# Folding the last two weights later, and splitting in halves, in a fused attention, gated MLP and bilinear MLP kernel

## The chip, the cores and the metric

The kernel runs on one core of one Trainium2 chip. The metric is the device time of one execution in microseconds (us); lower is better. A run's time is the median of several executions. A profile is one execution more, recorded instruction by instruction; its own time stands beside its span.

## The reference

```python
attn_out = _attn_ref(q, k, v)              # 4 batches, 8 heads, 576 positions, head size 64, window 128
x = attn_out.transpose(0, 2, 1, 3).reshape(2304, 512)
gate = 1.0 / (1.0 + np.exp(-(x @ w_gate))) # w_gate, w_val: 512 x 1536
x = gate * (x @ w_val) @ w_out             # w_out: 1536 x 512
a, b = x @ w1, x @ w2                      # w1, w2: 512 x 1024
h = a * b @ w3                             # w3: 1024 x 1024
out = h @ w_out2                           # w_out2: 1024 x 512
```

All data is float32. The weights reach the kernel as float64 words and are rounded to float32 on the chip.

## The kernel before, in words

**Split operands.** Each matrix product is three TensorE passes over values split into a high part (a rounded copy that ScalarE makes, `act_copy`) and a low part (the rest). The low part is a subtraction on VectorE (`dve_lo`) or on GpSimd (`pool_lo`, line 86). A group "wsl", "gt", "tp", "tq", "t", "forms" or "xf" in the profile is such a pair.

**Stages.** From 0 to some 190 us the attention runs, with the first products of the first MLP laid between as fillers. Then the first MLP runs group by group: a group is two slices of 128 hidden columns, and for each group all five token blocks (128 or 512 tokens wide parts of `TILES`) are passed: `gv` makes gate and value products in four PSUM banks, ScalarE's tanh (line 337) reads the first two banks, VectorE's product (line 344, "g") reads the other two, and `down1` ("dn") multiplies by `w_out` one block later.

**The last group.** The last group passes the blocks in the order `LAST_ORDER`. After each block `FOLD_PLAN` says in letters what else is recorded: `c` converts one more weight piece, `f` records one unit of the fold, `x` one step of `x_forms`. The fold computes w3 times w_out2 once (16 units of 12 matmuls, "w3o", line 285), so that the second MLP needs one product less. `x_forms` makes sums and differences of the tokens of two blocks ("xf"): with them seven block products do the work of eight. The weight forms ("forms") are made per slice from 12 on in `form_sink`.

**Weights on their way.** A piece is loaded (`fetch`, "raw", two buffers in turn), rounded from float64 by one ScalarE and six VectorE instructions (`rounded`, lines 131 to 137), and either split into its place or, for pieces of `early`, stored to DRAM as float32 ("early32") and loaded again later at half the bytes. `W3_AHEAD` and `W3_LATER` name the pieces of w3 that go that way. Rounding buffers ("ca") come two in turn too, so a piece waits for the store of the piece before last.

**Second MLP.** For eight slices (12 to 19) and two pairs of blocks, `products` makes the seven products in two PSUM banks "pb" and "pd" and one "pc"; ScalarE copies partial sums out of "pb" (x, xa, xb) before TensorE may add to them again; `lone` does the block that has no pair. The forms of each slice are stored to DRAM by line 214 ("formd") on SyncE's queue and loaded again for the second pair.

**What sets the order.** Each engine runs its own list in order; the lists are made by a scheduler from the recorded program, its priorities and its own estimate of times. TensorE's, VectorE's and ScalarE's lists interleave the stages; a row in a list waits for its data and for the buffer it writes, and everything behind it on that engine waits too. DMA issues are rows of the list of the engine that issues them.

Of the kernel before, what the change touches and what calls it, by code (L numbers as in the profile page):

```python
# [9 lines left out]
F32 = mybir.dt.float32  # L10
# [3 lines left out]
AF = mybir.ActivationFunctionType  # L14
ALU = mybir.AluOpType
# [4 lines left out]
P = 128  # L20
# [14 lines left out]
FULL = 4000.0  # L35

LAST_ORDER = (4, 0, 1, 2, 3)
FOLD_PLAN = {4: "ccccc", 0: "ccc", 1: "cccccccccc", 2: "cfcfcfcf", 3: "cfxcfxcfxx", None: "xxxffccfccfcfcfcfcfcf"}

PAIRED = ((1, 2), (3, 4))  # L40
A21, A22, A11, A12, S1, S2, S3, S4 = range(8)
# [4 lines left out]
)  # L46

W3_AHEAD = (0, 1, 10, 11, 12, 13, 14, 15)
W3_LATER = (2, 3, 4, 5)


def bits(word):
# [4 lines left out]
def attn_moe_kernel(  # L57
# [14 lines left out]
    nc = tc.nc  # L72
    NPAIR = qt.shape[0]
    D = P // 2
    NF, NM, NC2 = w_gate.shape[0], w1.shape[0], w_out2.shape[0]
# [3 lines left out]
    def act_copy(dst, src):  # L79
        nc.scalar.activation(dst, src, AF.Copy)  # L80
# [2 lines left out]
        nc.vector.tensor_tensor(dst, src, hi.bitcast(F32), ALU.subtract)  # L83

    def pool_lo(dst, src, hi):
        nc.gpsimd.tensor_tensor(dst, src, hi.bitcast(F32), ALU.subtract)  # L86

    aligned = ctx.enter_context(tc.tile_pool(name="aligned", bufs=1, side="right"))
    aligned.tile([P, 8], F32, name="aligned")
# [5 lines left out]
    formd = dpool.tile([NM * P, 7 * 4 * P], F32, name="formd")  # L95
    outd = dpool.tile([NM * P, 2 * DM], F32, name="outd")
# [87 lines left out]
    forms = {}  # L184
# [3 lines left out]
    def form_sink(key, x):  # L188

        i, c = key  # L190
        x = x.rearrange("p (b c) -> p b c", b=2)
        if c == 0:
            forms[i] = formpools[i % 2].tile([P, 8, 2, 2 * P], F32R, name=f"forms{i}", tag=f"forms{i % 2}")
            half[i] = x
        w = forms[i]

        def split(at, src):
            hi, lo = w[:, at : at + 2, 0], w[:, at : at + 2, 1]
            act_copy(hi, src)
            pool_lo(lo, src, hi)  # L200

        split(A11 if c == 0 else A21, x)
        if c == 1:
            a = half.pop(i)
            s12 = spool.tile([P, 2, 2 * P], F32, name=f"s12_{i}", tag="cs")
            s34 = spool.tile([P, 2, 2 * P], F32, name=f"s34_{i}", tag="cs")
            nc.vector.tensor_tensor(s12[:, 0], x[:, 0], x[:, 1], ALU.add)
            nc.vector.tensor_tensor(s12[:, 1], s12[:, 0], a[:, 0], ALU.subtract)
            nc.vector.tensor_tensor(s34[:, 0], a[:, 0], x[:, 0], ALU.subtract)
            nc.vector.tensor_tensor(s34[:, 1], a[:, 1], s12[:, 1], ALU.subtract)  # L210
            split(S1, s12)
            split(S3, s34)
            r = (i - NF) * P
            nc.sync.dma_start(formd[r : r + P, :], w[:, 1:].rearrange("p b h c -> p (b h c)").bitcast(F32))

    def out_tile(i):
        if i % GF == 0:
# [46 lines left out]
    early += [((i, c), (w1, w2)[c][i - NF]) for i in groups[NF // GF + 2] for c in range(2)]  # L264
    early += [it for it in fold_src if it[0][0] == "w3" and it[0][1] in W3_LATER]
    late_n = len(early)
# [6 lines left out]
    def fold_items():  # L273
        sinks = dict(o2=wo2_sink, w3=w3_sink)
        return [(key, ahead.get(key, src), sinks[key[0]]) for key, src in fold_src]

    def fold():
        for u in range(2 * NM):
            m, c = divmod(u, 2)
            if c == 0:  # L280
                acc2 = mm_tile([P, DM], f"w3o{m}")
            for i in range(4):
                kk = 4 * c + i
                for wp, xp in PASSES:
                    nc.tensor.matmul(  # L285
                        acc2, w3s[u][:, wp, i * P : (i + 1) * P], wo2[kk][:, xp],
                        start=(kk == 0 and wp == 0 and xp == 0),
                        stop=(kk == NC2 - 1 and wp == 1),
                    )
            if c == 1:  # L290
                o = m2.tile([P, 2, DM], F32R, tag="gt", name=f"w3o{m}", bufs=4)
                nc.scalar.activation(o[:, 0], acc2, AF.Copy, scale=0.25)
                nc.vector.scalar_tensor_tensor(o[:, 1], acc2, 0.25, o[:, 0].bitcast(F32), ALU.mult, ALU.subtract)
                nc.sync.dma_start(outd[m * P : (m + 1) * P, :], o.rearrange("p h c -> p (h c)").bitcast(F32))
            yield


# [7 lines left out]
    def mm_tile(shape, name):  # L305
        mmturn[0] += 1
        return mmpools[mmturn[0] % len(mmpools)].tile(shape, F32, tag="mm", name=name)
# [81 lines left out]
    def x_forms(n):  # L389

        p, q = (acc[blk] for blk in PAIRED[n])
        b11, b21, b12, b22 = p[:, 0:2], p[:, 2:4], q[:, 0:2], q[:, 2:4]

        def split(j, src, lo):
            t = xf[n, j] = xpool.tile([P, 2, 2, TB], F32R, name=f"xf{n}_{j}", tag=PLACES[n][j])
            act_copy(t[:, 0], src)
            lo(t[:, 1], src, t[:, 0])

        def minus(to, x, y):
            nc.vector.tensor_tensor(to, x, y, ALU.subtract)  # L400

        split(B11, b11, pool_lo)
        yield
        split(B21, b21, pool_lo)
        yield
        split(B22, b22, dve_lo)
        yield
        minus(b12, b12, b11)
        split(T1, b12, pool_lo)
        yield  # L410
        minus(b22, b22, b12)
        split(T2, b22, dve_lo)
        yield
        minus(b11, b22, b11)
        split(T3, b11, pool_lo)
        yield
        minus(b21, b21, b22)
        split(T4, b21, dve_lo)
        yield
# [437 lines left out]
    for blk in LAST_ORDER:  # L857
        for _ in layer(groups[last1], blk):
            pass
        follow(FOLD_PLAN[blk])  # L860
    flush()
# [7 lines left out]
    queue[2:2] = first[0:2]  # L869
    follow(FOLD_PLAN[None])  # L870
    assert not queue and next(fold_it, None) is None
# [7 lines left out]
    def step(it):  # L879
        return next(it, None)  # L880

    downs = iter(())
    for n in range(len(PAIRED)):
        for g, grp in enumerate(second):
            final = n == 0 and g + 1 == len(second)
            for at, i in enumerate(grp):
                alone = lone(i) if n == 0 else iter(())
                if i == slices[-1] and n == 0:
                    xform = x_forms(1)
                for gap in products(n, i):  # L890
                    if gap:
                        step(downs)
                    if gap in (2, 3):
                        step(alone)
                    if i == slices[-1] and n == 0:
                        step(xform)
                if at:
                    for _ in downs:
                        pass
                convert(2)  # L900
                nxt = n * len(slices) + slices.index(i) + 2 - len(slices)
                if 0 <= nxt < len(slices):
                    again(slices[nxt])
            nxt = n * len(second) + g + 1
            if nxt < 2 * len(second):
                out_again(second[nxt % len(second)])
            downs = down2(n, grp)
            if final:
                for _ in range(5):
                    step(downs)  # L910
# [53 lines left out]
```

## Time and profile before

| | |
|---|---|
| median of 3 runs | 927.54 us (925.88 to 927.7) |
| the profiled execution | 927.45 us, its span 925.7 us |
| TensorE busy | 880.0 us, 95% of the span |
| VectorE, ScalarE, GpSimd busy | 667.7, 352.0 and 330.0 us |
| chain that ended last | TensorE 61%, VectorE 20%, DMA 6%, ScalarE 5%, GpSimd 4% |
| mean granted TensorE clock | 0.989 of full speed |

The profiled execution is 0.09 us below the median of the runs, so sums made from its rows are set against 927.45. The 1.75 us between the span and its time lie around the program.

### The profile page before, as it was taken

The page shows a single profiled execution, that of the slowest core. Times are in us where ns is not written, and L with a number is a line of the kernel's source. Part 1 is how long each engine was busy: PE and PEld are TensorE (multiplying, and loading weights), DVE is VectorE, ACT ScalarE, POOL GpSimd, SP SyncE. Part 2 cuts the span into 40 slices and gives each one's busy share as a digit, 9 for nine tenths or more (in the row PEclk, how much of TensorE's full clock was granted, in tenths as well). Part 3 has the DMA queues.
Part 4 walks back from the last instruction along what each step waited for, and adds up shares of the span by engine and source line. Part 5 has one row for each costly group of instructions (what it writes and reads, how often), then busy time and mean ns, then how long its engine had stood idle before and what let it go on. Part 6 is the DMA issues. An engine that isn't in the chain of part 4 may idle for free.

```text
span 925.7 us, 12453 instructions
## 1 busy us (share of the span) xinstructions
PE 880.0 (95%) x4432; PEld 716.4 (77%) x4432; DVE 667.7 (72%) x1126; ACT 352.0 (38%) x839; POOL 330.0 (36%) x360
## 2 busy tenths in 40 slices
PE   6778998999999999999999999989899999999998
PEld 4556775788878888888888888867688888888886
DVE  5979898538997995896798844972679956434444
ACT  6878666532323322422332333432443324122120
POOL 4767554542323312412411213230755446112121
PEclk9999899999999999999999999999999999999999
DMA  5445352133241341251235332237644432555332
GB/s 198 154 134 184 109 191 78 38 91 115 91 154 63 103 161 44 82 161 65 69 128 167 114 91 95 65 114 265 235 171 183 192 126 93 217 212 188 108 114 91
DMA packets 40622, 121.66 MB, mean 131 GB/s; under 512 B 4464, under 2 KB 6512, under 8 KB 38512
## 3 DMA queue, kind: packets, MB, share of 16 engines
q1 hardware_dynamic: 40416, 120.74, 38.1%
q8 instruction: 35, 0.57, 0.3%
q14 instruction: 27, 0.22, 0.1%
q10 hardware_dynamic: 144, 0.13, 0.0%
HBM read 88.34 MB, written 32.51 MB: 131 GB/s over the span
## 4 chain that ended last, share of the span: by engine, by line
PE 61%; DVE 20%; DMA 6%; ACT 5%; issue 4%; POOL 4%; SPq 0%; ACTq 0%; DVEq 0%; POOLq 0%
PE gv L320 22%; PE dn L361 11%; PE o L519 9%; PE pb L429 7%; PE pd L429 3%; PE w3o L285 2%; ACT sm L682 2%; PE pc L429 2%; DVE s L666 1%; DVE sm L669 1%; PE lone L493 1%; PE pv L723 1%; DVE mn L675 1%; DVE acc L400 1%; POOL wsl L86 1%
## 5 line engine op out<-in xcount | busy, mean ns | idle before, releaser
L320 PE MATMUL gv<-xth,wsl 128*128 128x512 f32 (+1 forms) x960 | 282.3, 372 | 1.7 <-DVE g L344 1.0
L320 PEld LDWEIGHTS gv<-xth,wsl 128*128 128x128 f32 x960 | 176.3, 191 | 37.0 <-issue 3.0
L320 PE MATMUL gv<-xtl,wsl 128*128 128x512 f32 (+1 forms) x480 | 177.9, 371 | 0.2 <-DVE xtl L83 0.2
L361 PE MATMUL dn<-gt,wsl 128*128 128x512 f32 (+1 forms) x720 | 157.4, 372 | 12.1 <-DVE xtl L83 5.3
L86 POOL TENSOR_TENSOR gt<-g,gt 128x512 fp32r<-128x512 f32 (+1 forms) x60 | 74.6, 1247 | 239.2 <-ACT gt L80 239.0
L361 PEld LDWEIGHTS dn<-gt,wsl 128*128 128x128 f32 x720 | 126.6, 190 | 37.7 <-issue 6.2
L320 PEld LDWEIGHTS gv<-xtl,wsl 128*128 128x128 f32 x480 | 91.6, 191 | 15.5 <-DVE xtl L83 0.9
L371 DVE TENSOR_TENSOR acc<-acc,dn 128x512 f32<-128x512 f32 (+1 forms) x120 | 73.0, 625 | 15.6 <-PE dn L361 15.6
L529 DVE TENSOR_TENSOR acc<-acc,o 128x512 f32<-128x512 f32 x54 | 36.9, 684 | 49.0 <-PE o L519 49.0
L80 ACT ACTIVATE gt<-g 128x512 fp32r<-128x512 f32 (+1 forms) x60 | 35.1, 587 | 78.6 <-DVE g L344 78.5
L682 ACT ACTIVATE sm<-sm,mn 128x128 f32<-128x128 f32 x144 | 55.8, 390 | 18.1 <-DVE mn L679 13.0
L344 DVE SCALAR_TENSOR_TENSOR g<-g,gv 128x512 f32<-128x512 f32 (+1 forms) x60 | 37.3, 627 | 29.8 <-PE gv L320 27.4
L429 PE MATMUL pb<-xf,forms 128*128 128x512 f32 x192 | 50.7, 396 | 4.4 <-ACT xa L80 4.3
L86 POOL TENSOR_TENSOR tp<-x,tp 128x512 fp32r<-128x512 f32 x16 | 21.3, 1334 | 93.5 <-ACT tp L80 61.7
L429 PE MATMUL pb<-xf,again 128*128 128x512 f32 x192 | 49.5, 393 | 0.0
L519 PE MATMUL o<-outw,tp 128*128 128x512 f32 x192 | 48.4, 391 | 0.7 <-POOL tp L86 0.7
L519 PE MATMUL o<-outw,tq 128*128 128x512 f32 x192 | 48.7, 391 | 0.0
L690 POOL TENSOR_SCALAR sm<-sm,su 128x128 f32<-128x128 f32 x72 | 32.4, 463 | 43.1 <-DVE su L686 35.8
L285 PE MATMUL w3o<-wo,w3s 128*128 128x512 f32 x192 | 46.4, 398 | 0.7 <-ACT w3s L80 0.7
L429 PEld LDWEIGHTS pb<-xf,forms 128*128 128x128 f32 x192 | 34.8, 188 | 12.2 <-ACT xa L80 4.9
L285 PEld LDWEIGHTS w3o<-wo,w3s 128*128 128x128 f32 x192 | 36.3, 190 | 10.0 <-ACT w3s L80 1.1
L337 ACT ACTIVATE g<-gv 128x512 f32<-128x512 f32 (+1 forms) x60 | 32.2, 544 | 30.5 <-PE gv L320 26.8
(804 smaller groups left out, 1561.1 us busy)
## 6 DMA issues: line engine op xcount, KB each, us to landing
formd<-forms SPq DMA_DIRECT2D x8, 1792.0 KB, 6.1
outw<-outd SPq DMA_DIRECT2D x16, 512.0 KB, 5.0
again<-formd SPq DMA_DIRECT2D x8, 1024.0 KB, 5.2
ldk<-in_k_dram SPq DMA_DIRECT2D x16, 320.0 KB, 3.9
ldv<-in_v_dram SPq DMA_DIRECT2D x16, 320.0 KB, 3.0
out_dram<-acc SPq DMA_DIRECT2D x18, 256.0 KB, 2.0
ldq<-in_q_dram SPq DMA_DIRECT2D x16, 256.0 KB, 4.1
outd<-w3o SPq DMA_DIRECT2D x8, 512.0 KB, 2.9
```

The costliest lines, as they stand in the source:

```text
L80: nc.scalar.activation(dst, src, AF.Copy)
L86: nc.gpsimd.tensor_tensor(dst, src, hi.bitcast(F32), ALU.subtract)
L285: nc.tensor.matmul(acc2, w3s[u][:, wp, i * P : (i + 1) * P], wo2[kk][:, xp], start=(kk == 0 and wp == 0 and xp == 0), stop=(kk == NC2 - 1 ...
L320: nc.tensor.matmul(ps, wsl[i][:, s, wp, kk * P : (kk + 1) * P], xs[blk][xp][:, kk], start=(kk == 0 and wp == 0 and xp == 0), stop=(kk == N ...
L344: nc.vector.scalar_tensor_tensor(pr, pr, 1.0, pss[i, 1], ALU.add, ALU.mult)
L361: nc.tensor.matmul(ps, wsl[i][:, 2, wp, m * P : (m + 1) * P], t[:, xp], start=n == 0, stop=n == 3 * len(grp) - 1,)
L371: nc.vector.tensor_tensor(a, a, ps, ALU.add)
L429: nc.tensor.matmul(ps, forms[i][:, a, wp, kk * P : (kk + 1) * P], xf[n, j][:, xp, kk], start=first and kk == 0 and (wp, xp) == PASSES[0], ...
L519: nc.tensor.matmul(ps, ts2[n, i][blk][:, xp, tt * P : (tt + 1) * P], outw[i][:, wp], start=k == 0, stop=k == 3 * len(grp) - 1,)
L529: nc.vector.tensor_tensor(a, a, ps, ALU.add)
L682: s["act"] = nc.scalar.activation(y, y, AF.Exp, bias=mn[:, j : j + 1], scale=1.0 / up, accum_out=su[:, j : j + 1])
L690: nc.gpsimd.tensor_scalar(y, y, su[:, j : j + 1], 1.0, ALU.mult, ALU.mult)
```

## The change

Five edits. `pool_lo` makes each GpSimd subtraction as two instructions over half the columns. Four more pieces of w3 (6 to 9) are rounded ahead, stored and loaded again, and `FOLD_PLAN` places conversions and fold units later: no fold unit stands any more between the third and the fourth wide block of the last group. `x_forms` works in halves of 512 columns, on all engines. The store of a slice's forms is issued from ScalarE's queue, after the fold's last copy (`folded`), when the slice's products are recorded. The store of a folded piece ("outd") is recorded one unit later.

```diff
-FOLD_PLAN = {4: "ccccc", 0: "ccc", 1: "cccccccccc", 2: "cfcfcfcf", 3: "cfxcfxcfxx", None: "xxxffccfccfcfcfcfcfcf"}
+FOLD_PLAN = {4: "cccc", 0: "cc", 1: "cccc", 2: "cccccccccccc", 3: "cfcfcfcfxxx", None: "xxxxfccfccfcfcfcfcfcfcfcfcff"}
...
-W3_LATER = (2, 3, 4, 5)
+W3_LATER = (2, 3, 4, 5, 6, 7, 8, 9)
...
     def pool_lo(dst, src, hi):
-        nc.gpsimd.tensor_tensor(dst, src, hi.bitcast(F32), ALU.subtract)
+        n = src.shape[1] // 2
+        for k in (slice(0, n), slice(n, 2 * n)):
+            nc.gpsimd.tensor_tensor(dst[:, k], src[:, k], hi[:, k].bitcast(F32), ALU.subtract)
...
             split(S3, s34)
-            r = (i - NF) * P
-            nc.sync.dma_start(formd[r : r + P, :], w[:, 1:].rearrange("p b h c -> p (b h c)").bitcast(F32))
+
+    def keep(i):
+        r = (i - NF) * P
+        nc.scalar.dma_start(formd[r : r + P, :], forms[i][:, 1:].rearrange("p b h c -> p (b h c)").bitcast(F32))
...
-                nc.scalar.activation(o[:, 0], acc2, AF.Copy, scale=0.25)
+                folded[m] = nc.scalar.activation(o[:, 0], acc2, AF.Copy, scale=0.25)
...
-                nc.sync.dma_start(outd[m * P : (m + 1) * P, :], o.rearrange("p h c -> p (h c)").bitcast(F32))
+                made.append((m, o))
+            if c == 0 or u == 2 * NM - 1:
+                for k, o in made:
+                    nc.sync.dma_start(outd[k * P : (k + 1) * P, :], o.rearrange("p h c -> p (h c)").bitcast(F32))
...
-            act_copy(t[:, 0], src)
-            lo(t[:, 1], src, t[:, 0])
+            for h in range(2):
+                act_copy(t[:, 0, h], src[:, h])
+                lo(t[:, 1, h], src[:, h], t[:, 0, h])
...
-            nc.vector.tensor_tensor(to, x, y, ALU.subtract)
+            for h in range(2):
+                nc.vector.tensor_tensor(to[:, h], x[:, h], y[:, h], ALU.subtract)
...
+                if n == 0:
+                    with tc.issue_after(folded[NM - 1].ins):
+                        keep(i)
```

What the edits make of the lists shows at three places. (Numbers behind a name are buffers.)

The first place is ScalarE's list after the last group's first block (block 4). "a_" is the first instruction of a rounding, g_4 the tanh of that block, gt_4 the high part of its product. Before:

```order
L131 ACTIVATE a_('ahead', 'w3', 5)_5073<-raw_('ahead', 'w3', 5)_5059 128x512
L337 ACTIVATE g_4_4823<-gv_4_0_4797 128x512
L337 ACTIVATE g_4_4825<-gv_4_0_4810 128x512
L80 ACTIVATE gt_4_4840<-g_4_4823 128x512
L80 ACTIVATE gt_4_4857<-g_4_4825 128x512
L80 ACTIVATE wo_0_5191<-raw_('o2', 0)_5071 128x512
L80 ACTIVATE wo_0_5191<-raw_('o2', 1)_5083 128x512
L337 ACTIVATE g_0_4979<-gv_0_0_4953 128x256
```

After:

```order
L133 ACTIVATE a_('ahead', 'w3', 6)_5283<-raw_('ahead', 'w3', 6)_5269 128x512
L348 ACTIVATE g_4_4909<-gv_4_0_4883 128x512
L348 ACTIVATE g_4_4911<-gv_4_0_4896 128x512
L133 ACTIVATE a_('ahead', 'w3', 7)_5295<-raw_('ahead', 'w3', 7)_5281 128x512
L80 ACTIVATE gt_4_4926<-g_4_4909 128x512
L133 ACTIVATE a_('ahead', 'w3', 8)_5405<-raw_('ahead', 'w3', 8)_5293 128x512
L80 ACTIVATE gt_4_4944<-g_4_4911 128x512
L133 ACTIVATE a_('ahead', 'w3', 9)_5417<-raw_('ahead', 'w3', 9)_5305 128x512
```

Four roundings now stand before, between and behind the tanh and the copies of that block, the first of them (behind that of piece 5) ahead of both tanh. VectorE's list after the change has, at the same place, the product g_4 behind the first steps of the rounding of piece 7:

```order
L139 TENSOR_TENSOR a_('ahead', 'w3', 6)_5283<-a_('ahead', 'w3', 6)_5283,s_('ahead', 'w3', 6)_5284 128x512
L134 TENSOR_SCALAR a_('ahead', 'w3', 7)_5295<-a_('ahead', 'w3', 7)_5295 128x512
L135 TENSOR_SCALAR a_('ahead', 'w3', 7)_5295<-a_('ahead', 'w3', 7)_5295 128x512
L355 SCALAR_TENSOR_TENSOR g_4_4909<-g_4_4909,gv_4_1_4913 128x512
L136 SCALAR_TENSOR_TENSOR a_('ahead', 'w3', 7)_5295<-raw_('ahead', 'w3', 7)_5281,a_('ahead', 'w3', 7)_5295 128x512
L137 TENSOR_SCALAR s_('ahead', 'w3', 7)_5296<-a_('ahead', 'w3', 7)_5295 128x512
L138 SCALAR_TENSOR_TENSOR s_('ahead', 'w3', 7)_5296<-raw_('ahead', 'w3', 7)_5281,s_('ahead', 'w3', 7)_5296 128x512
L134 TENSOR_SCALAR a_('ahead', 'w3', 8)_5405<-a_('ahead', 'w3', 8)_5405 128x512
L355 SCALAR_TENSOR_TENSOR g_4_4911<-g_4_4911,gv_4_1_4931 128x512
```

Before, both g_4 products stood directly behind the last step of piece 5.

The second place is where the fold begins. TensorE after the change, behind the last block's products (gv_3) and the third block's down products (dn_2):

```order
L292 MATMUL w3o_5577<-wo_3_5442,w3s_5469 128x512 x6
L292 MATMUL w3o_5577<-wo_6_5455,w3s_5469 128x512 x6
L292 MATMUL w3o_5615<-wo_0_5429,w3s_5572 128x512 x9
L292 MATMUL w3o_5615<-wo_3_5442,w3s_5572 128x512 x3
L292 MATMUL w3o_5615<-wo_3_5442,w3s_5590 128x512 x2
L372 MATMUL dn_3_0_5668<-gt_3_5517,wsl_4476 128x512 x3
L372 MATMUL dn_3_0_5668<-gt_3_5535,wsl_4491 128x512
L292 MATMUL w3o_5615<-wo_3_5442,w3s_5590 128x512 x4
```

Before, the first four units stood ahead of gv_3. VectorE's list up to the low part that the last row there needs (w3s_5590), after the change:

```order
L83 TENSOR_TENSOR xf_2_5663<-acc_2_1776,xf_2_5663 128x512
L413 TENSOR_TENSOR acc_2_1776<-acc_2_1776 128x512
L83 TENSOR_TENSOR xf_2_5663<-acc_2_1776,xf_2_5663 128x512
L413 TENSOR_TENSOR acc_1_1296<-acc_2_1776,acc_1_1296 128x512
L413 TENSOR_TENSOR acc_2_1776<-acc_2_1776 128x512
L83 TENSOR_TENSOR xf_4_5718<-acc_2_1776,xf_4_5718 128x512
L413 TENSOR_TENSOR acc_1_1296<-acc_2_1776,acc_1_1296 128x512
L83 TENSOR_TENSOR xf_4_5718<-acc_2_1776,xf_4_5718 128x512
L413 TENSOR_TENSOR acc_1_1296<-acc_1_1296,acc_2_1776 128x512 x2
L300 SCALAR_TENSOR_TENSOR w3o_5607<-w3o_5577,w3o_5607 128x512
L83 TENSOR_TENSOR xf_6_5734<-acc_1_1296,xf_6_5734 128x512 x2
L83 TENSOR_TENSOR w3s_5590<-raw_('w3', 3)_5472,w3s_5590 128x512
```

The halves of x_forms stand in a row there, ahead of the fold's fourth piece.

The third place is ScalarE's list at slice 13, after the change:

```order
L80 ACTIVATE forms_5995<-s_13_6004 128x2x256
L80 ACTIVATE forms_5995<-s_13_6005 128x2x256
L218 DMA formd<-forms_5995 128x3584
L80 ACTIVATE tp_12_6098<-x_0_12_6020 128x512
L80 ACTIVATE tq_12_6110<-xa_12_6021 128x512
L80 ACTIVATE x_0_13_6140<-pb_13_6138 128x512
```

The store of a slice's forms stands there now, ahead of the copies of the products; before it was a row of SyncE's list.

## Rows read from the trace of the kernel before

**Rows 1.** Busy time by stage: us, each engine (instructions), granted clock, DMA share, GB/s.
```profile
560.00:700.00 140.00, 132.23 (x594) 107.27 (x593) 92.71 (x133) 51.66 (x86) 52.07 (x36) 0.98 0.46 164
```

**Rows 2.** TensorE's waits, 560 to 700 us: total us, times, longest.
```profile
PE pb L429 <- ACT xa L80: 4.3, 2, 3.6
PE dn L361 <- DVE acc L371: 2.1, 1, 2.1
PE w3o L285 <- ACT w3s L80: 0.7, 1, 0.7
PE pd L429 <- POOL forms L86: 0.6, 1, 0.6
```

**Rows 3.** TensorE's timeline, 603 to 668 us: start, us, instruction, idle before.
```profile
606.43 2.93 PE L361 MATMUL dn<-gt,wsl 128*128 128x512 f32 x6 [2.06 <-DVE acc L371]
...
659.71 1.84 PE L429 MATMUL pb<-xf,forms 128*128 128x512 f32 x6 [3.58 <-ACT xa L80]
661.35 2.76 PE L429 MATMUL pc<-xf,forms 128*128 128x512 f32 x6
...
665.56 1.57 PE L429 MATMUL pb<-xf,forms 128*128 128x512 f32 x6
```

**Rows 4.** DMA issues, 480 to 665 us: KB, median us to landing.
```profile
_('ahead', 'w3', 5)_5059<-in_w_dram SPq DMA_DIRECT2D x1, 512.0 KB, 4.3
...
raw_('w3', 13)_5754<-early SPq DMA_DIRECT2D x1, 256.0 KB, 8.0
...
raw_('w3', 15)_5793<-early SPq DMA_DIRECT2D x1, 256.0 KB, 2.6
```

**Rows 5.** ScalarE's timeline, 494 to 562 us.
```profile
514.98 0.68 ACT L131 ACTIVATE _('ahead', 'w3', 5)_5073<-_('ahead', 'w3', 5)_5059 128x512 f32<-128x512 f32 x1 [1.38 <-DMA early<-_('ahead', 'w3', 3)_5049]
515.57 1.07 ACT L337 ACTIVATE g<-gv 128x512 f32<-128x512 f32 x2
```

**Rows 6.** SyncE's queue, 500 to 665 us.
```profile
516.04 0.33 SPq L119 DMA_DIRECT2D raw_('o2', 0)_5071<-early  x1
...
520.90 0.32 SPq L119 DMA_DIRECT2D raw_('o2', 1)_5083<-early  x1
```

**Rows 7.** VectorE's timeline, 494 to 562 us.
```profile
501.68 0.41 DVE L133 TENSOR_SCALAR _('ahead', 'w3', 2)_4941<-_('ahead', 'w3', 2)_4941 128x512 uint32<-128x512 uint32 x1
...
504.04 0.69 DVE L137 TENSOR_TENSOR _('ahead', 'w3', 2)_4941<-_('ahead', 'w3', 2)_4941,_('ahead', 'w3', 2)_4942 128x512 f32<-128x512 f32 x1
...
521.48 1.28 DVE L344 SCALAR_TENSOR_TENSOR g<-g,gv 128x512 f32<-128x512 f32 x2
```

**Rows 8.** TensorE's timeline, 500 to 576 us.
```profile
522.84 0.28 PE L320 MATMUL gv<-xth,wsl 128*128 128x256 f32 x1
...
528.59 5.63 PE L361 MATMUL dn<-gt,wsl 128*128 128x512 f32 x24
```

**Rows 9.** VectorE's timeline in the third stage of x_forms.
```profile
598.73 1.22 DVE L400 TENSOR_TENSOR acc<-acc,acc 128x1024 f32<-128x1024 f32 x1
...
601.60 3.24 DVE L400 TENSOR_TENSOR acc<-acc,acc 128x1024 f32<-128x1024 f32 x1
```

**Rows 10.** GpSimd's subtractions (line 86): ns least/median/most, first and last start.
```profile
L86 POOL TENSOR_TENSOR gt<-g,gt x60: 733/1296/1702, 57.0 to 589.9; 128x512 fp32r<-128x512 f32 x48, 128x256 fp32r<-128x256 f32 x12
```

**Rows 11.** VectorE beside such subtractions, and one with none beside it (142.24).
```profile
86.25 1.38 DVE L135 TENSOR_SCALAR s_(1, 2)_939<-a_(1, 2)_938 128x512 uint32<-128x512 uint32 x1
...
142.24 0.42 DVE L133 TENSOR_SCALAR a_('ahead', 3, 2)_1449<-a_('ahead', 3, 2)_1449 128x512 uint32<-128x512 uint32 x1
...
654.17 1.51 DVE L209 TENSOR_TENSOR s<-raw_(14, 0)_5861,raw_(14, 1)_5876 128x256 f32<-128x256 f32 x1
```

**Rows 12.** GpSimd's timeline beside the last row of 11.
```profile
653.92 1.48 POOL L86 TENSOR_TENSOR tp<-x,tp 128x512 fp32r<-128x512 f32 x1
655.36 1.45 POOL L86 TENSOR_TENSOR tq<-xa,tq 128x512 fp32r<-128x512 f32 x1
```

**Rows 13.** SyncE's queue, 500 to 665 us: what the stores of forms waited for.
```profile
SPq L214 <- POOL forms L86: 7.7, 3, 3.2
```

More of the change, by code (lines that the diff above doesn't have):

```diff
@@ L275, in fold_items @@
         return [(key, ahead.get(key, src), sinks[key[0]]) for key, src in fold_src]
+    folded = {}
     def fold():
+        made = []
         for u in range(2 * NM):
@@ L291, in fold @@
                 o = m2.tile([P, 2, DM], F32R, tag="gt", name=f"w3o{m}", bufs=4)
-                nc.scalar.activation(o[:, 0], acc2, AF.Copy, scale=0.25)
+                folded[m] = nc.scalar.activation(o[:, 0], acc2, AF.Copy, scale=0.25)
                 nc.vector.scalar_tensor_tensor(o[:, 1], acc2, 0.25, o[:, 0].bitcast(F32), ALU.mult, ALU.subtract)
-                nc.sync.dma_start(outd[m * P : (m + 1) * P, :], o.rearrange("p h c -> p (h c)").bitcast(F32))
+                made.append((m, o))
+            if c == 0 or u == 2 * NM - 1:
+                for k, o in made:
+                    nc.sync.dma_start(outd[k * P : (k + 1) * P, :], o.rearrange("p h c -> p (h c)").bitcast(F32))
+                made.clear()
             yield
```

## The prediction

> **What bounds the kernel now.** I read the busy times first: TensorE is busy for 95% of the span, so a change can only win what TensorE idles, or what it loses at a lower clock. Then I read TensorE's waits by stage. The stage that the edits rearrange, 560 to 700 us, has 132.23 us of work in 140 [rows 1], and its waits sum to 7.7 us: 4.3 us for the copy xa of a partial sum (3.6 of it in one piece), 2.1 us for VectorE's addition to acc, 0.7 for a piece of w3 and 0.6 for a form [rows 2]. Last I read the timeline behind the two long waits, since it shows a second loss. Six matmuls take 1.57 us undisturbed; the six behind the 2.06 us wait take 2.93, and the twelve behind the 3.58 us wait take 1.84 and 2.76 [rows 3]. That is 1.36 + 0.27 + 1.19 = 2.8 us more, and the stage's mean granted clock is 0.98 where it should be 1.00 [rows 1]. So TensorE loses 7.7 + 2.8 = **10.5 us** in this stage. This is the most that the later fold can return.
>
> **The change part by part.**
>
> *The fold later.* The same 192 matmuls of the fold and all products stay. From the third place in which the lists differ (TensorE) one sees that the fold is now almost one block of work, and the products of slice 12 come behind it. The wait for xa came from a copy that stood behind conversions of forms while TensorE had no filler; behind the changed fold the copies have lone, pc and the next slice's pb between them. The waits for pieces of w3 came from late loads: one took 8.0 us to land, with a store of forms (1.8 MB) in flight, where its like takes 2.6 [rows 4]. The store is now behind the fold. I take all 10.5 us as removed, and put what comes in their place below: **-10.5**.
>
> *Four pieces rounded ahead.* This is the edit that I trust least, because of the first place of the lists. Before, ScalarE started piece 5 at 514.98 and both tanh right behind, at 515.57 [rows 5]. Now piece 6 stands between. Its load can go out only where the buffer of piece 4 comes free. That is where the load of o2 0 went out before, 516.04, and the next buffer came free at 520.90 [rows 6]; a 512 KB load takes 4.3 us to land [rows 4]. So piece 6 is there at 520.3; with 0.68 us for its first instruction and 1.07 for both tanh [rows 5] the tanh are done at 522.1 instead of 516.6. The 256-column block starts at 522.84 [rows 8], and its first two PSUM banks are free by then. The other two banks are freed by VectorE's products g_4, which ran at 521.48 [rows 7] and now stand behind the first steps of piece 7. Piece 7 lands at 520.9 + 4.3 = 525.2, its ScalarE step ends at 525.9, two VectorE steps of some 0.4 (the row without a neighbour) [rows 11] and g_4 (half of 1.28) [rows 7] end at 527.2. The 256-column block takes 528.59 - 522.84 = 5.75 us, 1.44 for each of four products [rows 8], so TensorE wants the third bank at 525.7: it waits 1.5 us. The fourth bank hangs on piece 8 in the same way: the buffer of piece 6 is free when its rounding has read it, some 3 us (501.68 to 504.73) [rows 7] behind 521.0, so it is loaded at 524.0 and lands at 528.3, and the second g_4 ends near 530.1; TensorE wants it at 528.6: 1.5 us more. Against this, halved subtractions may let VectorE come to this point 0.7 us earlier. I take 2.5 us of waits and 0.5 for a slower restart, **+3.0** (0 if the loads land 1.5 us sooner each, 5 if each wait costs a restart as dear as that in rows 3). What the later loads of o2 and w3 lose there is covered by two more blocks of some 11 us each before the fold.
>
> *x_forms in halves, ahead of the fold's fourth piece.* This crunch stays; the 2.06 us wait of before was its work. From the end of dn_2, TensorE has 38 fold matmuls and 4 of dn_3 before it needs the low part w3s_5590 (second place): 42 x 0.23 us (1.57 us for six is 0.39 for the last and 0.23 to 0.24 between starts) [rows 3] = 9.6 us. VectorE has its last addition and the 14 instructions shown, 15 x 0.61 = 9.2 us (0.61 is half of the 1.22 us row) [rows 9]. Meanwhile GpSimd makes four halves of xf_5, each 0.73 us [rows 10], and the two hold each other up: the 1.22 us instruction took 3.24 beside a GpSimd subtraction [rows 9]. With four such holds, 2.9 us less what overlaps with a wait, VectorE is at 11.7: a wait of some 2.2 us (0 without any hold, 3 with all), and 1.3 for the restart as in rows 3: **+3.5** (0 to 4.5).
>
> *Behind the fold.* A piece of w3 behind the forms of slice 12, and a first down product that asks for the low part of slice 13 early, can cost some tenths each: **+1.0** (0 to 2), with 0.6 as the size of the nearest wait [rows 2].
>
> *Halved subtractions elsewhere.* Two halves take 2 x 0.73 against 1.29, so 0.15 us more each [rows 10]. From 200 to 560 us TensorE does not wait for them, since a product's low part is used one block later; at the end of the program the last low part is waited for: **+0.2**. In the attention they help: VectorE's small instruction takes 0.42 alone and 1.38 beside a subtraction [rows 11]. I count five such places before 190 us. A half is over 0.55 us sooner, which bounds the gain at 2.5 us; TensorE waits for VectorE in only some of these: **-1.0** (0 to -2.5). The Trainium skill (SBUF — State Buffer, Who interferes with whom) says that the pair of ports which VectorE and GpSimd share is held for a whole instruction and that the other engine blocks fully until then. By that rule the gain is the full 2.5 us on VectorE; the trace agrees as far as 1.38 against 0.42 shows it, and the sum keeps 1.0.
>
> The store of "outd" a unit later costs nothing: nothing reads it for some 40 us.
>
> **Sum.** -10.5 + 3.0 + 3.5 + 1.0 + 0.2 - 1.0 = -3.8 us on 927.45: **923.6 us**, 0.4% faster.
>
> **The rivals.** *The new waits are hidden* (0.20): the loads land before the banks are wanted, or VectorE keeps ahead of GpSimd. Against it stand the 4.3 us of such loads and the 3.24 us row. Then 3 to 6.5 of the 6.5 us fall away: 917 to 920.5.
>
> *The gain is given back where the pieces are rounded* (0.16): each of pieces 6 to 9 costs a load's landing in front of a tanh or a product, some 1.5 us and a restart each, and x_forms at its upper bound: +7.5 and +4.5, within 0.2% of before (925.6 to 929.3).
>
> *ScalarE stands behind the stores* (0.19), slower: the store of a slice's forms is now a row of ScalarE's list ahead of the copies of the products (third place), and it waits for GpSimd's last subtraction. On SyncE's queue such stores waited 7.7 us in three times, 3.2 at most [rows 13], and nothing hung on it. GpSimd has six subtractions of two halves and a short one per slice, some 9.6 us; TensorE's eight block products and lone parts take some 11 us where no down product stands between. By my count the copy xb of slice 14 comes 1.4 us before TensorE needs it. If GpSimd is later than that, each such copy costs what xa's did, 3.58 + 1.46 = 5.0 us [rows 3]; one such copy gives 928.6 and from the second it decides: 933.6. The Trainium skill (Perfetto Trace Analysis, DMA Instruction — HWDGE (DVE, Sync)) says that the DMA engines do not wait on semaphores themselves, so the issuing engine stands; the 7.7 us on SyncE's queue agree with it.
>
> *Halving does not shorten VectorE's waits*, since GpSimd's second half takes the ports again: against it, VectorE's instruction from 654.17 to 655.68 got its turn between two subtractions that followed each other without a gap [rows 11, 12]. It would cost 1.0 to 1.5: 924.9, inside the forecast.
>
> **How the numbers follow.** The forecast's own case has 0.45: 921.5 to 925.5. Under 0.2% (1.9 us) a measurement of this kernel tells no change. Faster by more than that: 0.45 + 0.20 = 0.65; same 0.16; slower 0.19. The range, 917.5 to 930, leaves out the ends of the first and most of the last rival.
>
> **What would show it.** Right: no wait for xa of 3 us behind the fold; two waits of 1 to 2 us of TensorE's gv for VectorE's g near 525 to 531; a wait of w3o for w3s at the fold's fourth unit near 595; VectorE rows beside GpSimd's halves under 1.0 us in the attention. Wrong: no waits near 525 (then 917 to 920), or waits of pb for xa or xb above 2 us at slices 13 to 16 (then slower).

## The result: slower by 0.7%, and the profile after

| | median | range | runs |
|---|---|---|---|
| the kernel before | 926.71 us | 924.5 to 927.7 | 4 |
| the changed kernel | 933.02 us | 931.87 to 934.56 | 4 |

The ratio is 1.0072, with a 95% interval of 1.0048 to 1.0097. The forecast was 923.6 us with a range of 917.5 to 930: wrong in sign, and the time lies outside the range. The profiled execution has a span of 931.2 us against 925.7. (Line numbers of the changed kernel are up to 13 higher: `pool_lo` is line 88, the copies of `act_copy` stay at line 80.)

The first view to read again is busy time by stage, as in [rows 1]:

```profile
500.00:560.00 60.00, 57.01 (x283) 47.99 (x282) 45.78 (x82) 20.73 (x38) 12.73 (x16) 1.00 0.49 150
560.00:600.00 40.00, 37.85 (x159) 30.58 (x159) 23.64 (x34) 15.76 (x26) 19.90 (x24) 0.96 0.08 30
600.00:700.00 100.00, 98.88 (x471) 81.24 (x470) 52.49 (x87) 35.56 (x64) 42.30 (x58) 1.00 0.56 201
700.00:800.00 100.00, 91.38 (x426) 74.59 (x425) 70.51 (x110) 32.90 (x61) 56.85 (x70) 0.97 0.45 168
```

The stage that the edits were about holds more work now: from 560 to 700 us TensorE is busy for 136.73 us, where it was 132.23 [rows 1]. The loss lies behind it. TensorE is busy for 91.38 us of 700 to 800; in the kernel before it was 99.18:

```profile
700.00:800.00 100.00, 99.18 (x483) 82.54 (x483) 71.86 (x105) 33.69 (x56) 46.03 (x31) 1.00 0.45 168
```

TensorE's waits of the changed kernel, first from 500 to 690 us, then from 690 us to the end, show what it stands for:

```profile
PE gv L331 <- DVE g L355: 3.0, 2, 2.5
PE w3o L292 <- DVE w3s L83: 2.2, 1, 2.2
PE w3o L292 <- ACT w3s L80: 0.4, 1, 0.4
...
PE pb L442 <- ACT x L80: 2.7, 1, 2.7
PE pb L442 <- ACT xa L80: 2.6, 2, 1.8
PE o L532 <- POOL tp L88: 2.6, 1, 2.6
PE pd L442 <- DVE xb L477: 0.6, 1, 0.6
PE pb L442 <- ACT xb L80: 0.6, 1, 0.6
```

The first two rows are the two waits that the forecast had named and priced. Nothing in its sum stands for the five rows of the second window. Most of them are copies that ScalarE makes late, so the next view is ScalarE's timeline there:

```profile
735.91 0.33 ACTq L218 DMA_DIRECT2D formd<-forms  x1
736.28 0.60 ACT L80 ACTIVATE xa<-pb 128x512 f32<-128x512 f32 x1 [6.73 <-POOL forms L88]
```

ScalarE did nothing for 6.73 us. The row of the store itself shows only 0.33 us; its wait appears as the idle time of the copy xa behind it, "<-POOL forms". The Trainium skill (Perfetto Trace Analysis, DMA Instruction — HWDGE (DVE, Sync)) says that the profiler starts such a row when its semaphores are satisfied, so that a wait is not part of it; this trace agrees, with 0.33 beside 6.73. What ScalarE waited for is in GpSimd's timeline of the same moment, and what came of it in TensorE's:

```profile
724.06 0.89 POOL L88 TENSOR_TENSOR t<-g,t 128x128 fp32r<-128x128 f32 x2 [8.80 <-ACT t L80]
...
729.72 1.81 POOL L88 TENSOR_TENSOR forms<-s,forms 128x256 fp32r<-128x256 f32 x2
731.48 2.06 POOL L88 TENSOR_TENSOR tq<-xa,tq 128x256 fp32r<-128x256 f32 x2
733.50 2.37 POOL L88 TENSOR_TENSOR forms<-s,forms 128x256 fp32r<-128x256 f32 x2
```

```profile
736.93 2.12 PE L442 MATMUL pb<-xf,forms 128*128 128x512 f32 x6 [1.85 <-ACT xa L80]
```

GpSimd works without a pause from 724.06 (the three rows left out are of the same slice) and ends the last half of the form at 735.87, 11.8 us later; the store goes out at 735.91, xa is copied at 736.28, TensorE goes on at 736.93 and takes 2.12 us for six matmuls that take 1.56 when nothing has stopped it. Over 630 to 760 us the rows of ScalarE's waits add up to 28.0 us that it stood for forms at six stores:

```profile
ACT xa L80 <- POOL forms L88: 15.7, 3, 6.7
ACT xb L80 <- POOL forms L88: 9.5, 2, 5.8
ACT tp L80 <- POOL forms L88: 2.8, 1, 2.8
```

### The profile page after: what moved, and what is told of

The parts are those of the page before. It is cut to its first block, busy times and chain, and to the rows that moved or that the text cites. A ratio compares the mean times of both kernels' runs of the same rounds, so it can differ in the third digit from the quotient of the medians.

```text
span 931.2 us, 12708 instructions
## 1 busy us (share of the span) xinstructions
PE 881.1 (95%) x4432; PEld 716.8 (77%) x4432; DVE 648.9 (70%) x1140; ACT 353.3 (38%) x853; POOL 380.2 (41%) x552
## 4 chain that ended last, share of the span: by engine, by line
PE 60%; DVE 22%; POOL 6%; issue 5%; ACT 4%; DMA 3%; ACTq 0%; DVEq 0%; POOLq 0%
PE gv L331 22%; PE dn L372 12%; PE o L532 8%; PE pb L442 6%; PE w3o L292 3%; PE pd L442 3%; POOL forms L88 2%; PE pv L736 2%; DVE s L679 2%; DVE sm L682 2%; ACT sm L695 2%; PE pc L442 2%; DVE mn L688 1%; PE pt L713 1%; DVE acc L382 1%
## 5 line engine op out<-in xcount | busy, mean ns | idle before, releaser
L88 POOL TENSOR_TENSOR gt<-g,gt 128x256 fp32r<-128x256 f32 (+1 forms) x120 | 95.6, 819 | 213.5 <-ACT gt L80 213.5
L88 POOL TENSOR_TENSOR tp<-x,tp 128x256 fp32r<-128x256 f32 x32 | 25.6, 822 | 102.7 <-ACT tp L80 70.1
L532 PE MATMUL o<-outw,tp 128*128 128x512 f32 x192 | 50.6, 402 | 2.7 <-POOL tp L88 2.6
L532 PEld LDWEIGHTS o<-outw,tp 128*128 128x128 f32 x192 | 36.8, 194 | 12.1 <-POOL tp L88 3.5
```

The lines of the kernel that those rows point to most:

```text
L88: nc.gpsimd.tensor_tensor(dst[:, k], src[:, k], hi[:, k].bitcast(F32), ALU.subtract)
L532: nc.tensor.matmul(ps, ts2[n, i][blk][:, xp, tt * P : (tt + 1) * P], outw[i][:, wp], start=k == 0, stop=k == 3 * len(grp) - 1,)
```

## The experiments

Two theories stood against each other. **A**: ScalarE stands at the stores, and the copies behind them come late. **B**: GpSimd is itself late, because two halves take longer than a whole (its busy time rose from 330.0 to 380.2 us), and the stores matter little. Each ratio is to the kernel before, timed beside it; in microseconds a difference of 0.001 is 0.93.

| run | fold | GpSimd's halves | stores issued from | median us | ratio (95%) |
|---|---|---|---|---|---|
| the change | later | everywhere | ScalarE | 933.02 | 1.0072 (1.0048 to 1.0097) |
| e1_sync_store | later | everywhere | SyncE | 922.61 | 0.9949 (0.9928 to 0.9969) |
| e2_whole | later | none | ScalarE | 935.35 | 1.0079 (1.0056 to 1.0103) |
| e3_sync_whole | later | none | SyncE | 929.23 | 1.0018 (1.0002 to 1.0033) |
| e4_before_halved | before's | everywhere | SyncE | 923.49 | 0.9960 (0.9947 to 0.9974) |
| e5_before_act_store | before's | none | ScalarE | 930.24 | 1.0032 (1.0016 to 1.0047) |
| e6_act_store_later | later | everywhere | ScalarE, behind tq | 925.70 | 0.9977 (0.9960 to 0.9995) |
| e7_sync_round_later | later, lists as e1 | everywhere | SyncE | 921.87 | 0.9940 (0.9919 to 0.9962) |
| e8_sync_old_plan | before's | everywhere | SyncE | 919.98 | 0.9930 (0.9903 to 0.9956) |
| e9_whole_second | later | to the first MLP | ScalarE | 926.70 | 0.9995 (0.9980 to 1.0011) |
| e10_pool_store | later | everywhere | GpSimd | 925.29 | 0.9977 (0.9959 to 0.9995) |
| e11_late_sync | later | everywhere | ScalarE to slice 15 | 927.00 | 0.9996 (0.9980 to 1.0013) |
| e12_act_old_plan | before's | everywhere | ScalarE | 923.18 | 0.9952 (0.9934 to 0.9970) |
| e13_act_behind_xb | later | everywhere | ScalarE, behind xb | 921.81 | 0.9945 (0.9930 to 0.9959) |
| e14_sync_whole_second | later | to the first MLP | SyncE | 922.14 | 0.9942 (0.9924 to 0.9961) |

**e1_sync_store: the stores on SyncE's queue again.**

```diff
-        nc.scalar.dma_start(formd[r : r + P, :], ...)
+        nc.sync.dma_start(formd[r : r + P, :], ...)
```

> The changed kernel with one line undone: the store of a slice's forms is issued from SyncE's queue again, at the place in the program where the change put it. Theory A (ScalarE stands behind the stores, and the copies xa, xb and x behind them come late): the waits of pb for xa and xb between 695 and 740 us (0.59, 0.74, 0.64 and 1.85 us in the changed kernel) and the slow matmuls behind them go, 4 to 7 us in all, so 926 to 929 us. Theory B (GpSimd itself is late, because each halved subtraction takes longer, and ScalarE stands on buffers that GpSimd frees as well): the 2.74 us wait for x near 708 and the 2.58 us wait for tp near 792 stay, the gain is under 3 us, 930 to 933 us.

It gained 11.4 us (1.0072 against 0.9949, give or take 3), more than A expected, and is faster than both kernels. TensorE's waits from 500 us on are the four of the first window below and one behind it:

```profile
PE w3o L292 <- DVE w3s L83: 2.2, 1, 2.2
PE gv L331 <- DVE g L355: 2.0, 2, 1.5
PE pb L442 <- ACT x L80: 0.9, 1, 0.9
PE w3o L292 <- ACT w3s L80: 0.8, 2, 0.5
...
PE o L532 <- POOL tp L88: 0.9, 1, 0.9
```

The stores still wait for GpSimd, even longer, but on a queue behind which nothing of TensorE's hangs (SyncE's queue, 630 to 760 us):

```profile
SPq L218 <- POOL forms L88: 38.5, 7, 7.7
```

So B falls as the main cause: GpSimd's busy time is the same (379.6 us), and yet the 2.7 us for x near 708 are gone and the 2.6 for tp fell to 0.9. From 500 us on TensorE's waits add up to 6.8 us, 14.7 in the change: 7.9 of the 11.4 us. The rest was not itemised; the granted clock of 700 to 800 us is 1.00 in e1 and 0.97 in the change.

The edit moved more than the queue. With the stores out of ScalarE's list the scheduler made other lists from some 620 us on: some 25 of ScalarE's rows, 50 of VectorE's and 80 matmuls stand elsewhere, the two roundings of slice 16, for example, ahead of a copy xb instead of behind it and the store of slice 15. So the 11.4 us are the price of the stores together with the order that came with them. e11 below tells them apart in part.

**e2_whole, e3_sync_whole, e4_before_halved: the halves.**

```diff
     def pool_lo(dst, src, hi):
-        n = src.shape[1] // 2
-        for k in (slice(0, n), slice(n, 2 * n)):
-            nc.gpsimd.tensor_tensor(dst[:, k], src[:, k], hi[:, k].bitcast(F32), ALU.subtract)
+        nc.gpsimd.tensor_tensor(dst, src, hi.bitcast(F32), ALU.subtract)
```

> The changed kernel with GpSimd's subtractions in one instruction over all columns again; the stores stay on ScalarE's queue and x_forms stays in halves of 512 columns. Theory A: the stores still stand ahead of the copies, so most waits of 695 to 740 us stay, and the 2 us won in the attention is lost: 930 to 935 us. Theory B: GpSimd's busy time falls by some 40 us to near 335, it ends a slice's forms 1 to 3 us sooner, the store waits that much less, and the waits of 695 to 740 and the one of 2.58 us near 792 go; less the 2 us of the attention, 923 to 928 us.

> Both edits undone in the changed kernel: stores from SyncE's queue, GpSimd's subtractions whole. The rest (fold later, four more pieces rounded ahead, x_forms in halves) is as in the change. By both theories nothing of the loss behind 690 us is left; by the terms that the trace of the changed kernel bears out (-10.5 for the fold, +3 near 525, +3.5 near 593) it is 921 to 925 us. If it stays above 928, neither the stores nor the halves are the cause, and the loss behind 690 us comes from the order that the later fold leaves there.

> The kernel before with one edit: GpSimd's subtractions in halves of the columns, everything else as before. Theory A: only the attention changes, 1 to 2.5 us faster, 924 to 926 us. Theory B: GpSimd's busy time rises by some 40 us, forms and token forms come later, and TensorE waits for them in the stage of the last group and the first pair of the second MLP: 3 to 6 us slower less 2 in the attention, 928 to 931 us.

In these three runs the lists of TensorE, VectorE and ScalarE are those of the kernel that each was made from (for e3, of e1). e2 and e4 came out within 0.6 us of A's ranges. e3 did not: it is above 928, where I would have put the blame on the order that the later fold leaves. But its loss is not there: TensorE is busy for 97.98 us of 700 to 800 in e3, 91.38 in the change. What e3 lacks beside e1, 6.4 us, are the gains of the halves, which I had put at 2. Alone, in the kernel before, the halves gain 3.7 us.

**e9_whole_second, e14_sync_whole_second: halves in attention and first MLP only**, `forms`, `xf`, "t", "tp" and "tq" whole again.

```diff
+    def pool_whole(dst, src, hi):
+        nc.gpsimd.tensor_tensor(dst, src, hi.bitcast(F32), ALU.subtract)
...
-            pool_lo(lo, src, hi)
+            pool_whole(lo, src, hi)
```

> The changed kernel with GpSimd's subtractions whole in the second MLP alone (weight forms, token forms, products); attention and first MLP keep the halves; stores on ScalarE's queue. Theory E (halving costs behind the stores, since ScalarE stands until the last half is done): the gain of the halves up to the last group, 4 us between the runs of the change with and without halves, is kept, and the 2 us that the halves add behind it go: 929 to 932 us. Theory F (halving is of no account there, and the 2 us are chance of one trace): 932 to 935 us.

> The change with stores on SyncE's queue and GpSimd's subtractions whole in the second MLP alone; attention and first MLP keep the halves. If halves hurt in the second MLP only because ScalarE stands behind them at the stores, they cost nothing here and the time is that of halves everywhere with SyncE's stores within 1.5 us: 921 to 924 us. If the halves help in the second MLP too, by shorter waits of VectorE, it is 925 to 928 us; if they hurt there by GpSimd's longer busy time alone, 918 to 921 us.

With e1 to e3 these make a table of two edits:

| halves | SyncE's stores | ScalarE's stores | cost of the stores |
|---|---|---|---|
| everywhere | 0.9949 | 1.0072 | 11.4 us |
| up to the first MLP | 0.9942 | 0.9995 | 4.9 us |
| none | 1.0018 | 1.0079 | 5.7 us |

Each cost of the stores is give or take 3 us, so 11.4 stands clear of the other two, which are alike. Halves in the second MLP cost nothing with SyncE's stores, as e14's first case had it, and 7.1 us with ScalarE's. e9 is faster than both its theories allowed, 926.70 us where E ended at 929. ScalarE's 28.0 us at the stores are 6.9 for xb, 12.3 for xa and 2.6 for tp in e9, 21.8 us in all.

**e5_before_act_store, e8_sync_old_plan, e12_act_old_plan: the fold's plan.** e5 is the kernel before with ScalarE's stores; e8 and e12 are e1 and the change with the old `FOLD_PLAN` and `W3_LATER`.

> The kernel before with one edit: the stores of the forms are issued from ScalarE's queue, recorded with the slice's products, everything else as before (GpSimd's subtractions whole, fold early). Theory A (the store in ScalarE's list, ahead of the copies of the slice before, costs by itself): with whole subtractions it costs what it costs between the two runs of the change with whole subtractions, 5 to 7 us: 931 to 935 us. Theory C (the store costs only behind the later fold or with halves): within 2 us of the kernel before.

> The change with stores on SyncE's queue, with the fold's plan and the list of pieces rounded ahead of the kernel before; halves of GpSimd's subtractions and of x_forms stay. My terms for the later fold in the prediction are -10.5 + 3.0 + 3.5 + 1.0, of which the 3.5 stand for x_forms too; without them the fold's waits for xa and acc come back: 925 to 928 us. If the later fold is worth little because its waits only change places, 921 to 925 us.

> The changed kernel with the fold's plan and the list of pieces rounded ahead of the kernel before; halves and stores on ScalarE's queue as in the change. If the stores cost 10 us or more by themselves with halves, whatever the fold does: 929 to 933 us (with stores on SyncE's queue the same plan took 920). If it takes the later fold to make them that dear, as the 3.4 us of the stores alone in the kernel before suggest: 922 to 926 us.

e5 lies between its two theories: the stores alone cost the kernel before 3.0 us (1.5 to 4.4). With the old plan and halves they cost 2.0 us (e12 against e8, give or take 3), not 11.4, the second case of my expectation. And e8, faster than both its cases, takes away the gain that I had put on the later fold: with the old plan the time is not above that of e1 (0.9930 and 0.9949; the intervals overlap). One thing that differs between the plans shows in ScalarE's list. In the change (with TensorE's row that waits for the copy):

```profile
706.15 0.63 ACT L80 ACTIVATE forms<-a_(17, 1)_6594 128x512 fp32r<-128x512 f32 x1 [2.07 <-DVE a_(17, 1)_6594 L139]
707.29 0.63 ACT L80 ACTIVATE tq<-xa 128x512 fp32r<-128x512 f32 x1 [0.50 <-DVE xa L492]
707.82 0.58 ACT L80 ACTIVATE x<-pb 128x512 f32<-128x512 f32 x1
...
708.46 1.65 PE L442 MATMUL pb<-xf,forms 128*128 128x512 f32 x6 [2.74 <-ACT x L80]
```

In e12, with the other plan:

```profile
702.08 0.58 ACT L80 ACTIVATE x<-pb 128x512 f32<-128x512 f32 x1
705.49 0.63 ACT L80 ACTIVATE forms<-a_(17, 1)_6582 128x512 fp32r<-128x512 f32 x1 [2.83 <-DVE a_(17, 1)_6582 L139]
```

Both lists hold a row that waits for the rounding of piece (17, 1), late in both. In the change the copy x stands behind it and TensorE waits 2.74 us at 708.46; in e12 x stands ahead, and TensorE waits 1.2. How much of the gap between 11.4 and 2.0 this one difference makes up was not tried.

**e6_act_store_later, e13_act_behind_xb, e10_pool_store, e11_late_sync: where the store stands.**

In e6 (`turned` holds the copies tq; e13 has `taken`, the copies xb, in its place):

```diff
-                    with tc.issue_after(folded[NM - 1].ins):
+                    with tc.issue_after(folded[NM - 1].ins), tc.issue_after(turned[0, i].ins):
```

e10 has `nc.gpsimd` in the line of e1's diff, e11 `(nc.sync if i >= 16 else nc.scalar)`.

> The changed kernel with the store still on ScalarE's queue, but a slice later in its list: behind the copy tq of the same slice's products, so that GpSimd has made the whole form before ScalarE comes to the store. Theory A (it is ScalarE standing for GpSimd that costs): ScalarE no longer waits for forms at the stores, and the time is that of the change with stores on SyncE's queue, 921 to 924.5 us. Theory D (it is the queue itself: stores of 1.8 MB issued from ScalarE, or SyncE's loads running beside them): it stays at 928 to 934 us.

> The changed kernel with the store on ScalarE's queue, behind the copy xb of the same slice's products: all three copies of that slice out of pb are then ahead of the store, and the store is some 5 us earlier in the list than behind tq. If it is the copies standing behind a store that waits for GpSimd that cost, no copy waits for forms by way of the store, and of the waits for the store's own transfer (5.72 and 2.59 us behind tq) at most 2 us are left: 921 to 925 us. If the stores cost on ScalarE's queue wherever they stand, 926 to 933 us.

> The changed kernel with the store of a slice's forms issued from GpSimd's own queue, behind its last subtraction of that slice. Theory A (the wait of ScalarE for GpSimd is what costs): no engine stands for another at the store, so the time is near that with stores on SyncE's queue, 921 to 925 us; the copies xa, xb and x are not late. If issuing the store takes GpSimd itself several us, its forms come late and it is 925 to 931 us.

> The changed kernel with the stores of slices 16 to 19 on SyncE's queue and those of 12 to 15 still on ScalarE's. The trace of the changed kernel puts the waits at 695 to 740 us, where the stores of slices 16 to 18 stand: 921 to 925 us. If the stores of slices 12 to 15, where ScalarE waited 3.76 and 5.76 us without TensorE waiting at once, set off the lateness that shows later, 926 to 931 us.

e13 has no wait at a store for GpSimd's forms any more, and is as fast as e1 with the stores still on ScalarE. Its lists are e1's but for some 20 rows each of ScalarE and VectorE and 7 matmuls. So it isn't the queue; it is where in the list the store stands. (One wait of 2.7 us for x stays in its trace, behind forms that waited for VectorE.) e6 puts the store later still, lands between its two theories (925.70 us) and gets a new wait: the next form that is written into the same buffer must wait for the store to have read it. ScalarE's timeline in e6, and what TensorE waited for:

```profile
710.25 0.63 ACT L80 ACTIVATE forms<-a_(17, 0)_6579 128x512 fp32r<-128x512 f32 x1 [5.72 <-DMA formd<-forms]
710.79 0.58 ACT L80 ACTIVATE xa<-pb 128x512 f32<-128x512 f32 x1
```

```profile
PE pb L443 <- ACT xa L80: 5.5, 2, 4.4
```

In e10 no copy is late either, but the time, 925.29 us, is just in its slower range, and not for that range's reason: a store took GpSimd itself 0.77 us at most. The store of slice 12 (1.8 MB) went out at 613.46, in the middle of the fold; a piece of w3 that was loaded beside it kept ScalarE waiting for 7.2 us and TensorE for 2.6. e11 is the run closest to the change: ScalarE's list is the change's but for its last four stores and one rounding (VectorE has some 15 rows elsewhere, TensorE 9). It is 7.0 us faster (give or take 3), so with the order kept ScalarE's stand at the stores of slices 16 to 19 costs this much by itself. The other 4.4 of the 11.4 us stay, 2.74 of them in one wait for x near 710, as in the change. Whether the stores of slices 12 to 15 make them or the order was not tried apart; both meet in one row. ScalarE stood 5.76 us at the store of slice 15 and began the rounding of piece (16, 0) behind it at 680.15; in e1 (the last row), where that rounding stands further ahead and waits only for its load, it is at 667.61:

```profile
679.35 0.60 ACT L80 ACTIVATE xb<-pb 128x512 f32<-128x512 f32 x1 [5.76 <-POOL forms L88]
...
680.15 0.66 ACT L133 ACTIVATE a_(16, 0)_6400<-raw_(16, 0)_6239 128x512 f32<-128x512 f32 x1
```

```profile
667.61 0.67 ACT L133 ACTIVATE a_(16, 0)_6400<-raw_(16, 0)_6239 128x512 f32<-128x512 f32 x1 [3.48 <-DMA raw_(16, 0)_6239<-in_w_dram]
```

Behind it the forms of slice 16 and the roundings of slice 17 come late in e11 too, though SyncE issues their stores.

**e7_sync_round_later: two roundings recorded two blocks later** (`4: "cc", 1: "cccccc"` in `FOLD_PLAN`).

> The change with stores on SyncE's queue, and two of the conversions that stood behind the last group's first block (4) recorded behind its third (1) instead. If the 2.0 us of waits of gv for g near 525 come from the roundings that stand ahead of g_4, they fall to under 1 us and the time to 920 to 922 us; if the later roundings then delay the pieces of the fold, a wait of w3o takes their place and the time is 922 to 925 us.

The letters changed and the lists did not: in the trace of e7 every engine's rows stand in the order of e1's. So e7 is e1 measured once more (0.9940 beside 0.9949, and 2.1 us of waits of gv for g beside 2.0), and whether the roundings ahead of g_4 make that wait stays untried.

## Why the prediction was wrong

**The failed step** is the one that the prediction set aside as its slower rival, "ScalarE stands behind the stores": the sum held nothing for the stores on ScalarE's list. They cost 11.4 us (e1), more than the whole difference to the kernel before. The rival's mechanism was right, with its place (waits for xa and xb behind the stores), but two of its numbers were not. I put GpSimd's work for a slice at 9.6 us, from halves of 0.73 us that nothing disturbs [rows 10]; at slice 18 it took 11.8 us, since beside VectorE the pairs took 1.81, 2.06 and 2.37 us instead of 1.46. And I looked at slice 14 alone, where the copy had 1.4 us in hand; other stores held ScalarE longer: 2.85, 3.76 and 5.76 us at slices 13 to 15, 3.59 at 17, 6.73 at 18 and 5.4 at 19. That one stand makes the next high parts and roundings late, and so the next form, is read from the rows of e11 and was not tried alone. The rival's 933.6 us lie near the measured 933.02 by luck: they were two copies at 5.0 us each, and the trace has no wait above 2.7 us there.

**The later fold, -10.5 + 3.0 + 3.5 + 1.0.** The waits came where they were put: 3.0 us of gv for g (predicted 2.5 and a restart), 2.2 for w3s at the fold's fourth unit (predicted 2.2), 0.4 behind it (1.0 with what follows). But the first came by another chain, and its size is in part luck: two waits of 0.5 and 2.5 us where I had 1.5 twice, the 256-column block 3.3 us sooner than in the sum (519.57), and piece 8 loaded by 524.8 where I had 528.3. What each of the pieces 6 to 8 waited for last was the store of the rounded piece before last, as the row of piece 8 shows:

```profile
525.52 0.66 ACT L133 ACTIVATE _('ahead', 'w3', 8)_5405<-_('ahead', 'w3', 8)_5293 128x512 f32<-128x512 f32 x1 [1.77 <-DMA early<-_('ahead', 'w3', 6)_5283]
```

From 500 to 700 us TensorE worked 1.5 us more than before (193.74 against 192.23) where the terms give 3.0. But measured against the same kernel with the old plan the later fold is worth nothing (e8 to e1: +1.8 us, give or take 3). The 10.5 us were read in a kernel with whole subtractions, and there it is worth nothing either: e3, which has the later fold and `x_forms` in halves with whole subtractions and SyncE's stores, is 1.7 us slower than the kernel before (1.0018). So the step that failed here is the price of what comes in place of the 10.5 us. In e3 TensorE's waits over 500 to 690 us are

```profile
PE gv L329 <- DVE g L353: 3.8, 2, 2.0
PE w3o L290 <- DVE w3s L83: 2.7, 1, 2.7
PE pb L440 <- ACT x L80: 1.2, 1, 1.2
PE w3o L290 <- ACT w3s L80: 1.1, 2, 0.7
```

8.8 us, where [rows 2] add up to 7.7 and the prediction had put 4.7 of new waits, 1.8 of restarts and 1.0 behind the fold. With halves the old plan waits less too; e8's are

```profile
PE pb L442 <- ACT xa L80: 2.5, 3, 1.7
```

and four more, 6.9 us in seven waits, none above 1.7, where [rows 2] had one of 3.6; and the granted clock of 600 to 700 us is 1.00 in e8, 0.97 before. e1 loses 5.9 us there. From TensorE's first 256-column block (near 520 us) to its first product of the second pair it takes 270.44 us before, 271.52 in e3, 267.99 in e4, 266.61 in e8, 266.09 in e1 and 279.69 in the change.

**The halves, -1.0 and +0.2.** Right in kind, too small: 3.7 us in the kernel before (e4), and 7.0 behind the later fold (e3 to e14). In the traces, whose spans are 5.8 us apart, TensorE is 2.9 us ahead in e4 at the block near 520 us (519.94 against 522.84); another 2.4 us lie between that block and the second pair, where I had counted none. The row that was 1.38 us in [rows 11] is now

```profile
86.35 0.83 DVE L137 TENSOR_SCALAR s_(1, 2)_945<-a_(1, 2)_944 128x512 uint32<-128x512 uint32 x1
87.22 1.11 DVE L138 SCALAR_TENSOR_TENSOR s_(1, 2)_945<-raw_(1, 2)_745,s_(1, 2)_945 128x512 f32<-128x512 uint32 x1
```

under 1.0, as I had asked for; the row behind it is not, with 1.11 us where it took 0.74 before. The two rows alone would prove little. But VectorE's busy time fell from 667.7 to 648.9 us, and to 650.9 in e4, with the same work. So the rival "halving does not shorten VectorE's waits" is out.

**The sum by the runs**, each step from one ratio to the next: halves -3.7 (e4), halves of `x_forms` with the later records of the stores -2.8 (e8, give or take 3), the later fold +1.8 (e1), ScalarE's stores, with the order that came with them, +11.4: +6.7 us, which is 1.0072. Without ScalarE's stores the forecast, 923.6 us, would have been met (e1, 922.61), and by luck: the later fold, which was to give 3.0 us, gave none, and the halves, put at 0.8, gave 3.7 (e4).

## What to carry to other kernels

A DMA issue is a row of its engine's list: before a store is moved to an engine, list what stands behind it there and who waits for that, and follow it over several rounds of the loop, since an engine that stands can make late what the other engine needs for the next store. The same store was free behind the last copy of its slice (e13), cost 11.4 us ahead of the copies, and cost again one step later, when its buffer was wanted (e6). Where a scheduler makes the lists, compare them before and after an edit: here moving one DMA also moved some 150 other rows, and one edit of the plan moved none (e7). And price what a rearrangement brings as carefully as what it removes: 7.7 us of waits went, and 8.8 came (e3).

## What the runs showed of the hardware

Halves of a GpSimd subtraction give VectorE its turn between them, and this is paid by GpSimd: the subtractions "gt" in e2, whole, and in the change, in halves (count, busy time, mean ns of one, idle before), took

```profile
L86 POOL TENSOR_TENSOR gt<-g,gt 128x512 fp32r<-128x512 f32 (+1 forms) x60 | 74.6, 1246 | 235.5 <-ACT gt L80 235.3
```

```profile
L88 POOL TENSOR_TENSOR gt<-g,gt 128x256 fp32r<-128x256 f32 (+1 forms) x120 | 95.6, 819 | 213.5 <-ACT gt L80 213.5
```

and so 21.0 us more in all. From e2 to the change, which differ in the halves alone, GpSimd's busy time rose by 49.3 us over the kernel and VectorE's fell by 17.8. The Trainium skill (SBUF — State Buffer, Who interferes with whom) calls the pair of ports that the two share an exclusive lock; the traces agree as far as the row of 1.38 us beside a whole subtraction and of 0.83 beside a half shows it, and [rows 11, 12] add that VectorE's instruction gets in between two GpSimd instructions that follow each other.

What a wait costs TensorE beside its length did not follow the length: after 2.74 us without work (708.46) six matmuls took 1.65 us, after 1.85 us (736.93) they took 2.12, where 1.56 for six is usual. The granted clock (the third number from the end) was full, 2.4 GHz, behind the longer wait; behind the shorter one it was 0.74, so that part of those 4 us ran at the lower level, 1.2 GHz:

```profile
708.00:712.00 4.00, 3.54 (x18) 3.03 (x19) 3.93 (x6) 2.72 (x5) 4.00 (x5) 1.00 0.60 231
736.00:740.00 4.00, 3.07 (x9) 2.48 (x10) 1.83 (x4) 2.02 (x4) 0.00 (x0) 0.74 0.86 362
```
